# An attention and gated-convolution kernel: one list of operations put in another order from its 149th entry on

## The chip, the cores and the metric

The kernel runs on one core of one Trainium2 chip. The metric is the device time of one execution in microseconds; a kernel's time is the median of its runs. The profiler takes one execution and gives for it a span and, for each instruction, an engine, a start and a duration.

## The reference

Eight batches, eight heads, a sequence of 576 and a head dimension of 64 go through an attention without softmax, a norm over the head dimension, and then a feed-forward block with a depthwise convolution of three taps as its gate. All inputs and the output are float32; the output is 8 x 576 x 512.

```python
kv = np.einsum('bhsd,bhse->bhde', k, v)
out = np.einsum('bhsd,bhde->bhse', q, kv)
rms = np.sqrt(np.mean(out * out, axis=-1, keepdims=True) + 1e-06)
x = out / rms * g_norm                  # then (B, S, H * D) = (8, 576, 512)
...
h = np.maximum(x @ w_in, 0.0)           # 512 -> 1024
for k in range(3):                      # hp: h with a zero row at each end
    conv_out += conv_w[k][None, None, :] * hp[:, k:k + S, :]
gate = 1.0 / (1.0 + np.exp(-conv_out))
y = h * gate @ w_out                    # 1024 -> 512
```

## The kernel before

The kernel has no loop over batches. Some sixty small functions (lines 246 to 777) each issue one step of the work for one batch, half or tile, and a string `ORDER` (lines 59 to 134, 852 tokens) lists the steps. The end of the kernel walks through the list and then ties the instructions of each engine to that order, so that no scheduler moves them:

```python
    for token in ORDER.split():
        what, _, at = token.partition("@")
        slots[:] = [int(s) for s in at.split(",")] if at else []
        name, *args = what.split(".")
        ops[name](*(int(a) if a.isdigit() else a for a in args))
```

A token is a step's name, its arguments, and behind an `@` the places it takes: the PSUM bank (of eight, each 128 x 512 float32; attention steps take two neighbours) or the buffer of a ring. `on.2.1.0@0` is the norm sum of batch 2, head group 1, half 0 of the sequence, in banks 0 and 1. Each engine works through its own instructions in the order of the list; an instruction waits until its inputs are there and until the last reader of its place is done. So the list sets the order of each engine, and the numbers behind `@` set which earlier work a step has to wait for.

The steps of one batch, with the lines under which the profile shows them:

- Loads of q, k and v on GpSimd's queue (`Lq`, `Lk`, `Lv`, L347), each 576 KB and some in two parts.
- On TensorE with quarter arrays (64 x 64): the product of k and v (`kv` L402, 72 matmuls; `kz` L479 for batches 6 and 7), the transposes of q (`qt` L433, 36 matmuls) and the output product (`ot` L460, 4 matmuls; `ox` L500). For batches 6 and 7 q is transposed by a transfer on SyncE's queue instead (`tq` L467), and two transfers swap the halves of the k-v product (`kx` L489). A transfer of this kind stands in SyncE's queue with the stores.
- The copies out of PSUM: `kvd`, `qd` on VectorE (L414, L443), `kva`, `qa` on ScalarE (L416).
- The norm: squares on ScalarE (`sq` L509), the sum over the head dimension as a product with ones on TensorE, either on the whole array (`on` L528, 2 matmuls) or on quarter arrays (`oq` L537, 4 matmuls), the reciprocal root on ScalarE (`nl` L545), and the scaling into x on VectorE (`mo` L556). Batches 4 to 7 take a grouped form (`ss` L566, `ln` L574, `sl` L581 to L584, `sp` L593, `mu` L599) with a copy of the output (`oc` L521).
- The first product of the feed-forward block on TensorE (`hm` L613, `hs` L628, `hk` L658) and its relu on ScalarE (`re` L619, `rh` L640, `rp` L665).
- The gate: two scaled copies and two sums on VectorE (`ta` L681 and L682, `aa` L687, `ab` L692), the sigmoid on ScalarE (`sg` L698), the product with h on VectorE (`mg` L722). Batch 0 takes part of it on TensorE (`cv` L708).
- The second product, two batches at a time in nine tiles of 128 rows (`om` L732; the last tile `oh` L757), the copy of a tile's row out of its bank on ScalarE (`ea` L738, `eh` L767) or VectorE (`ed` L743), and its store on SyncE's queue (`st` L748, `sh` L777).

ScalarE needs one table for the reciprocal root and another for the sigmoid; where the list goes from one to the other, a table load stands in ScalarE's order (L227, ten in all).

In the code the two forms of the norm sum differ in this:

```python
    def on(b, u, s):                                        # L523
        ...
            nc.tensor.matmul(ps[:, tt, :], ones, T["sq", b, u, s][:, tt, :], start=True, stop=True)
    def oq(b, u, s):                                        # L531
        ...
                c = half(i)
                nc.tensor.matmul(
                    ps[c, tt, :], ones[c, c], T["sq", b, u, s][c, tt, :], start=True, stop=True)
```

Of the kernel before, what the change touches and what calls it, by code (L numbers as in the profile page):

```python
# [71 lines left out]
sq.1.0.0@5 hk.0.7.1.0@6 hk.0.7.1.1 rp.7.1 ta.0.1.7@1 ot.1.1.1@0 sq.1.1.1@6 oq.1.0.0@4 nl.1.0.0@5 mo.1.0.0 hk.0.4.0.0@6
hk.0.4.0.1 rp.4.0 hk.0.6.1.0@7 hk.0.6.1.1 rp.6.1 oq.1.1.1@4 nl.1.1.1@6 mo.1.1.1 hk.0.6.0.0@6 Lq.2.0.4@2 hk.0.6.0.1
rp.6.0 ta.0.1.4 hk.1.6.1.0@7 ta.0.1.6 hk.1.0.1.0@2 ot.1.1.0@4 sq.1.1.0@7 aa.0.1.2 hk.1.1.1.0@3 hk.1.2.1.0@6 hk.1.6.1.1
rh.1.6.1 hk.1.1.1.1 rh.1.1.1 on.1.1.0@0 nl.1.1.0@7 mo.1.1.0 hk.1.2.1.1 hk.1.5.1.0@7 hk.1.5.1.1 rh.1.5.1 rh.1.2.1
hk.1.3.1.0@3 hk.1.3.1.1 rh.1.3.1 hk.1.0.1.1 rh.1.0.1 ab.0.1.2 sg.0.1.5 sg.0.1.4 qt.2.1.0@0 qt.2.0.0@6 hk.1.5.0.0@3
hk.1.5.0.1 rh.1.5.0 qd.2.0.0@4 hk.1.0.0.0@2 hk.1.4.1.0@4 hk.1.4.1.1 hk.1.0.0.1 hk.1.1.0.0@5 hk.1.6.0.0@6 hk.1.1.0.1
hk.1.2.0.0@7 hk.1.2.0.1 rh.1.2.0 rh.1.1.0 rh.1.0.0 hk.1.6.0.1 rh.1.6.0 aa.0.1.3 qd.2.1.0@0 ab.0.1.3 sg.0.1.7 sg.0.1.6
hk.1.7.0.0@0 mg.0.1.2 hk.1.7.1.0@1 hk.1.7.1.1 rh.1.7.1 hk.1.7.0.1 rh.1.7.0 ta.1.1.1@0 ta.1.1.0 Lk.2.0.4@1 Lv.2.0.4@0
Lq.3.0.4@0 Lk.3.0.4@0 Lv.3.0.4@1 Lq.4.0.4@1 aa.1.1.0 hk.1.4.0.0@3 om.0.1.0.4@2 rh.1.4.1 hk.1.4.0.1 rh.1.4.0  # L80
om.0.2.0.4@5 kv.2.0.2@6 mg.0.1.3 om.0.1.4.4 ab.1.1.0 sg.1.1.0 sg.1.1.1 kvd.2.0.2@2 ot.2.0.1@0 sq.2.0.1@0 ed.0.1@0
st.0.1 qt.3.1.0@6 qd.3.1.0@1 Lk.4.0.4@1 Lv.4.0.4@0 Lq.5.0.4@2 om.0.2.4.4 on.2.0.1@2 qt.3.0.0@6 qd.3.0.0@2 nl.2.0.1@8
mo.2.0.1@2 om.0.3.0.4@4 ea.0.2@1 ot.2.1.1@6 ot.2.1.0@2 mg.1.1.0 om.0.3.4.4 ed.0.3@2 sq.2.1.0@1 sq.2.1.1@2 on.2.1.0@0
nl.2.1.0@9 mo.2.1.0 om.0.0.0.4@5 hk.1.3.0.0@4 on.2.1.1@0 st.0.2 nl.2.1.1@0 mo.2.1.1 om.0.0.4.4 ed.0.0@3 ot.2.0.0@2
sq.2.0.0@3 hk.1.3.0.1 rh.1.3.0 st.0.0 kv.3.0.2@0 kvd.3.0.2@0 on.2.0.0@6 nl.2.0.0@1 mo.2.0.0 hs.2.0.1@4 rh.2.0.1@1
hs.2.5.1@5 rh.2.5.1 ot.3.1.1@0 sq.3.1.1@4 ta.1.1.5@1 ot.3.0.1@6 sq.3.0.1@5 hs.2.1.1@4 rh.2.1.1 hs.2.4.0@5 rh.2.4.0
ta.1.1.4 ta.1.1.2@0 pn hs.2.4.1@2 rh.2.4.1 hs.2.1.0@3 rh.2.1.0 on.3.1.1@4 nl.3.1.1@2 hs.2.2.0@2 rh.2.2.0 hs.2.5.0@3
rh.2.5.0 on.3.0.1@4 nl.3.0.1@3 aa.1.1.2 mo.3.1.1@0 hs.2.2.1@2 rh.2.2.1 hs.2.0.0@3 rh.2.0.0 ot.3.0.0@0 sq.3.0.0@6
mo.3.0.1 qt.4.0.0@4 qd.4.0.0@3 ta.1.1.3 ab.1.1.2 aa.1.1.1 ot.3.1.0@2 sq.3.1.0@7 hs.2.3.1@6 rh.2.3.1 on.3.0.0@4
nl.3.0.0@4 hs.3.4.1@7 rh.3.4.1 hs.3.1.1@6 rh.3.1.1 on.3.1.0@4 nl.3.1.0@5 mo.3.0.0 hs.3.6.1@7 rh.3.6.1 hs.2.6.0@6  # L90
mo.3.1.0 qt.5.0.0@4 qd.5.0.0@0 ab.1.1.1 qt.4.1.0@0 qd.4.1.0@4 sg.1.1.5 sg.1.1.4 Lq.6.0.4@0 mg.1.1.2 ta.1.1.6@1
ta.1.1.7 aa.1.1.3 hs.2.3.0@7 rh.2.3.0 hs.3.0.1@2 rh.3.0.1 rh.2.6.0 sg.1.1.3 sg.1.1.2 hs.3.7.0@3 hs.3.2.0@4 rh.3.2.0
hs.3.3.0@5 rh.3.3.0 rh.3.7.0 kv.4.0.2@0 kvd.4.0.2@1 hs.3.0.0@2 hs.3.3.1@6 mg.1.1.1 Lk.5.0.4@0 rh.3.3.1 hs.3.2.1@7
rh.3.2.1 hs.3.7.1@4 rh.3.7.1 hs.3.6.0@5 rh.3.6.0 rh.3.0.0 ab.1.1.3 ta.2.2.2@0 ta.2.2.3 hs.3.4.0@3 rh.3.4.0 sg.1.1.7
hs.3.1.0@4 hs.3.5.0@5 sg.1.1.6 rh.3.1.0 qt.5.1.0@0 qd.5.1.0@2 ot.4.0.0@6 sq.4.0.0@0 mg.1.1.3 rh.3.5.0 om.0.7.0.4@2
# [729 lines left out]
```

## Time and profile before

| | |
|---|---|
| timed runs | 177.69, 177.48, 177.60 us; median 177.6 |
| profiled execution, span | 175.6 us (no time of its own is given beside the span) |
| instructions | 5070 |
| TensorE, matmul | 167.9 us busy, 96% |
| TensorE, weight load | 100.0 us, 57% |
| VectorE | 149.5 us, 85% |
| ScalarE | 148.9 us, 85% |
| GpSimd | 22.2 us, 13% |
| DMA | 29.11 MB, mean 166 GB/s |

The shares are means over stages that differ. Up to about 120 us attention and feed-forward work are mixed, with loads up to about 93 us; behind that there is feed-forward work alone, and stores. In the profile's tables a row names the line, the engine, the operation and the tile, then the number of instructions, their busy time, the mean of one in ns, and the idle time ahead of them with what ended it ("issue" is time in which the engine waited for nothing that the profile shows). In a timeline a row gives start, duration, engine, line, and how many instructions are drawn together.

### The profile page before, as it was taken

The page shows a single profiled execution, that of the slowest core. Times are in us where ns is not written, and L with a number is a line of the kernel's source. Part 1 is how long each engine was busy: PE and PEld are TensorE (multiplying, and loading weights), DVE is VectorE, ACT ScalarE, POOL GpSimd, SP SyncE. Part 2 cuts the span into 40 slices and gives each one's busy share as a digit, 9 for nine tenths or more (in the row PEclk, how much of TensorE's full clock was granted, in tenths as well). Part 3 has the DMA queues.
Part 4 walks back from the last instruction along what each step waited for, and adds up shares of the span by engine and source line. Part 5 has one row for each costly group of instructions (what it writes and reads, how often), then busy time and mean ns, then how long its engine had stood idle before and what let it go on. Part 6 is the DMA issues. An engine that isn't in the chain of part 4 may idle for free.

```text
span 175.6 us, 5070 instructions
## 1 busy us (share of the span) xinstructions
PE 167.9 (96%) x2097; PEld 100.0 (57%) x2114; DVE 149.5 (85%) x290; ACT 148.9 (85%) x268; POOL 22.2 (13%) x35
## 2 busy tenths in 40 slices
PE   7979999999999999999999999999999999999992
PEld 2334766676447677644467764444877744444451
DVE  2796638899688899999999998989999999999950
ACT  2368899999978999999999998999999967676721
POOL 3094512200603013030000000000000000000000
PEclk9999999999999999999999999999999999999999
DMA  5999999999999999999999050330310003064486
GB/s 159 392 323 207 207 207 207 208 208 209 207 241 230 227 207 207 170 182 197 258 181 161 14 134 0 119 123 0 119 63 0 0 0 116 13 239 175 179 304 237
DMA packets 25911, 29.11 MB, mean 166 GB/s; under 512 B 6036, under 2 KB 20384, under 8 KB 25888
## 3 DMA queue, kind: packets, MB, share of 16 engines
q0 software_dynamic: 13296, 14.50, 49.2%
q1 hardware_dynamic: 12048, 13.11, 26.2%
q10 hardware_dynamic: 544, 1.18, 1.7%
q8 instruction: 16, 0.26, 0.6%
q14 instruction: 7, 0.06, 0.1%
HBM read 32.52 MB, written 9.44 MB: 239 GB/s over the span
## 4 chain that ended last, share of the span: by engine, by line
PE 76%; DVE 12%; ACT 5%; DMA 3%; issue 3%; ACTq 0%; DVEq 0%
PE banks L732 32%; PE banks L628 14%; PE banks L613 9%; PE banks L658 4%; DMA stg<-in_v_dram 3%; PE banks L460 3%; DVE h L722 2%; PE banks L708 2%; ACT taps L698 2%; PE banks L402 2%; PE banks L593 2%; PE banks L433 1%; PE banks L528 1%; DVE taps L681 1%; PE banks L286 1%
## 5 line engine op out<-in xcount | busy, mean ns | idle before, releaser
L732 PE MATMUL banks<-w_out_sb,h 128*128 128x512 bf16 x267 | 62.8, 379 | 1.2 <-issue 0.6
L698 ACT ACTIVATE taps<-taps,cw 128x576 bf16<-128x576 bf16 (+1 forms) x44 | 40.6, 958 | 5.7 <-DVE taps L692 5.5
L732 PEld LDWEIGHTS <-h 128*128 128x128 bf16 x280 | 26.2, 98 | 30.0 <-issue 1.1
L628 PE MATMUL banks<-x,w_in_sb 128*128 128x288 bf16 (+2 forms) x256 | 34.2, 286 | 0.0
L640 ACT ACTIVATE h<-banks 128x288 bf16<-128x288 f32 (+2 forms) x80 | 29.5, 460 | 0.3 <-PE banks L658 0.2
L628 PEld LDWEIGHTS <-w_in_sb 128*128 128x128 bf16 x256 | 24.4, 98 | 7.8 <-issue 0.8
L722 DVE TENSOR_TENSOR h<-h,taps 128x1152 bf16<-128x1152 bf16 (+1 forms) x24 | 22.8, 952 | 1.2 <-ACT taps L698 1.2
L687 DVE TENSOR_TENSOR taps<-taps 128x1152 bf16<-128x1152 bf16 (+1 forms) x22 | 21.5, 978 | 0.5
L509 ACT ACTIVATE sq<-banks 128x576 bf16<-128x576 f32 (+2 forms) x32 | 20.8, 691 | 1.1 <-PE banks L460 1.1
L692 DVE TENSOR_TENSOR taps<-taps,h 128x1152 bf16<-128x1152 bf16 (+1 forms) x22 | 21.4, 972 | 0.3
L681 DVE TENSOR_SCALAR taps<-h,cw 128x576 bf16<-128x576 bf16 (+1 forms) x44 | 18.7, 424 | 0.6 <-ACT h L665 0.5
L682 DVE TENSOR_SCALAR taps<-h,cw 128x576 bf16<-128x576 bf16 (+1 forms) x44 | 18.4, 418 | 0.0
L738 ACT ACTIVATE row<-banks 128x512 f32<-128x512 f32 x23 | 13.5, 597 | 5.7 <-PE banks L732 4.2
L658 PE MATMUL banks<-x,w_in_sb 128*128 128x288 bf16 (+2 forms) x128 | 17.7, 286 | 0.1
L613 PE MATMUL banks<-x,w_in_sb 128*128 128x288 bf16 x128 | 16.9, 286 | 0.0
L556 DVE SCALAR_TENSOR_TENSOR x<-banks,cw,rs 128x576 bf16<-128x576 f32 (+2 forms) x16 | 13.0, 816 | 3.9 <-ACT rs L545 3.6
L658 PEld LDWEIGHTS <-w_in_sb 128*128 128x128 bf16 x128 | 12.0, 98 | 4.4 <-issue 0.5
L227 ACT ACT_TABLE_LOAD x10 | 12.8, 1283 | 2.0 <-issue 1.8
L613 PEld LDWEIGHTS <-w_in_sb 128*128 128x128 bf16 x128 | 12.3, 98 | 3.7 <-issue 0.2
L443 DVE COPY qT<-banks 128x1152 bf16<-128x1152 bf16 (+2 forms) x13 | 8.8, 681 | 5.7 <-PE banks L433 5.7
L545 ACT ACTIVATE rs<-banks,eps_sb 128x576 f32<-128x576 f32 (+2 forms) x16 | 11.8, 740 | 1.1 <-PE banks L528 1.1
L599 DVE SCALAR_TENSOR_TENSOR x<-o,cw,banks 128x576 bf16<-128x576 f32 (+2 forms) x16 | 12.1, 810 | 0.7 <-PE banks L593 0.5
(89 smaller groups left out, 162.9 us busy)
## 6 DMA issues: line engine op xcount, KB each, us to landing
out_dram<-row SPq DMA_DIRECT2D x35, 256.0 KB, 2.3
q_sb<-in_q_dram POOLq DMA_DIRECT2D x6, 576.0 KB, 17.9
k_sb<-in_k_dram POOLq DMA_DIRECT2D x6, 576.0 KB, 14.5
v_sb<-in_v_dram POOLq DMA_DIRECT2D x6, 576.0 KB, 17.9
stg<-in_v_dram ACTq DMA_DIRECT2D x2, 576.0 KB, 6.2
stg<-in_k_dram SPq DMA_DIRECT2D x4, 288.0 KB, 6.9
w_in_sb<-in_moe_w_in_dram POOLq DMA_DIRECT2D x2, 512.0 KB, 9.9
w_out_sb<-in_moe_w_out_dram POOLq DMA_DIRECT2D x1, 1024.0 KB, 15.5
```

Source lines behind the costliest of these rows:

```text
L509: nc.scalar.activation(T["sq", b, u, s], T["o", b, u, s], AX.Square)
L613: nc.tensor.matmul(ps[:, s, :HS], w_in_sb[:, t, f * P:(f + 1) * P], T["x", b][:, t, c0:c1], start=(t == 0), stop=(t == NT - 1))
L628: nc.tensor.matmul(ps, w_in_sb[:, t, f * P:(f + 1) * P], T["x", b][:, t, c0:c1], start=(t == 0), stop=(t == NT - 1))
L640: nc.scalar.activation(h, fr, AX.Relu)
L658: nc.tensor.matmul(T[at], w_in_sb[:, t, f * P:(f + 1) * P], T["x", b][:, t, c0:c1], start=(t == 0), stop=(t == NT - 1))
L681: nc.vector.tensor_scalar_mul(tap[:, 0, f % 2, :n, 8:8 + S], h[:, f], cw[:, f:f + 1])
L682: nc.vector.tensor_scalar_mul(tap[:, 1, f % 2, :n, :S], h[:, f], cw[:, 2 * NF + f:2 * NF + f + 1])
L687: nc.vector.tensor_add(tap[:, 1, :, :n, :S], tap[:, 0, :, :n, 7:7 + S], tap[:, 1, :, :n, 1:1 + S])
L692: nc.vector.tensor_add(y, y, span(b, n)[:, 2 * j:2 * j + 2])
L698: nc.scalar.activation(y, y, AX.Sigmoid, scale=cw[:, NF + f:NF + f + 1])
L722: nc.vector.tensor_mul(h, h, tap_of(b, j)[:, 1, :, :n, :S])
L732: nc.tensor.matmul(T["om", p, m], h[:, f, m * P:(m + 1) * P], w_out_sb[:, f, :], start=(f == 0), stop=(f == NF - 1))
```

## The change

The first 148 entries of the list are written in another order too, but give each engine the same row of steps, up to about 30 us. The entries behind them are put in another order that moves steps on every engine, and the numbers of banks and buffers are assigned anew. The functions and all line numbers stay. The steps themselves differ in a few places only: three norm sums change their form (`oq.1.0.0` and `oq.1.1.1` become `on`, `on.2.1.0` becomes `oq`), and eight tiles change the engine that copies them (`ea.0.2`, `ea.3.1` to VectorE's `ed` and, the other way, `ed.0.0`, `ed.1.8` and others; VectorE has 12 copies before and 10 after, ScalarE 23 and 25). One line of the list, of before and of after, from the end:

```diff
-mg.7.1.3 om.3.3.0.4@2 om.3.3.4.4 ed.3.3@5 st.3.3 mg.7.1.2 om.3.1.0.4@1 om.3.2.0.4@7 om.3.0.4.4 om.3.2.4.4 ed.3.2@0
+ea.3.0@4 st.3.0 st.3.1 st.3.2 sg.7.1.5 mg.7.1.2 om.3.7.4.4 ed.3.7@0 om.3.5.4.4 ea.3.5@1 om.3.4.4.4 ea.3.4@2 st.3.5
```

What this does to the engines' orders is shown at three places. The first is VectorE in batch 3's norm, from the first sum of one pair of gate taps of batch 1 (L687) to the gate product of that pair (L722, taps_73), before:

```order
L687 TENSOR_TENSOR taps_73<-taps_73 128x2x576
L556 SCALAR_TENSOR_TENSOR x<-banks,cw,rs 128x2x288 x2
L443 COPY qT<-banks 128x1152
L681 TENSOR_SCALAR taps_72<-h,cw 128x576
L682 TENSOR_SCALAR taps_72<-h,cw 128x576
L692 TENSOR_TENSOR taps_73<-taps_73,h 128x2x576
L687 TENSOR_TENSOR taps_72<-taps_72 128x2x576
L556 SCALAR_TENSOR_TENSOR x<-banks,cw,rs 128x2x288 x2
L443 COPY qT<-banks 128x1152
L692 TENSOR_TENSOR taps_72<-taps_72,h 128x2x576
L443 COPY qT<-banks 128x1152
L722 TENSOR_TENSOR h<-h,taps_73 128x2x576
```

and after:

```order
L687 TENSOR_TENSOR taps_73<-taps_73 128x2x576
L681 TENSOR_SCALAR taps_72<-h,cw 128x576
L682 TENSOR_SCALAR taps_72<-h,cw 128x576
L556 SCALAR_TENSOR_TENSOR x<-banks,cw,rs 128x2x288 x2
L692 TENSOR_TENSOR taps_73<-taps_73,h 128x2x576
L687 TENSOR_TENSOR taps_72<-taps_72 128x2x576
L556 SCALAR_TENSOR_TENSOR x<-banks,cw,rs 128x2x288
L692 TENSOR_TENSOR taps_72<-taps_72,h 128x2x576
L556 SCALAR_TENSOR_TENSOR x<-banks,cw,rs 128x2x288
L443 COPY qT<-banks 128x1152 x2
L722 TENSOR_TENSOR h<-h,taps_73 128x2x576
```

L556 is the scaling of a norm half into x, L443 the copy of transposed q, L681 and L682 the scaled copies of the gate, L692 its second sum. Before, the first two halves were scaled directly behind the first L687, and the copies of q stood between the pairs; now two gate copies stand ahead of them, the last two halves are scaled one by one with L692 between them, and two copies of q stand together ahead of the product.

The second place is TensorE in batch 2's norm: the norm sum L528 of one half, ahead of it the second product of the feed-forward block (L732). Before, from the last product on:

```order
L732 LDWEIGHTS h
L732 MATMUL banks<-w_out_sb,h 128x512
L658 LDWEIGHTS w_in_sb
L658 MATMUL banks<-x,w_in_sb 128x288
L658 LDWEIGHTS w_in_sb
L658 MATMUL banks<-x,w_in_sb 128x288
L528 LDWEIGHTS ones
L528 MATMUL banks<-sq,ones 128x288
L528 LDWEIGHTS ones
L528 MATMUL banks<-sq,ones 128x288
```

and after, from the sum of the half ahead on:

```order
L537 LDWEIGHTS ones
L537 MATMUL banks<-sq,ones 64x288
L732 LDWEIGHTS h
L732 MATMUL banks<-w_out_sb,h 128x512
L732 LDWEIGHTS h
L732 MATMUL banks<-w_out_sb,h 128x512
L732 LDWEIGHTS h
L732 MATMUL banks<-w_out_sb,h 128x512
L732 LDWEIGHTS h
L732 MATMUL banks<-w_out_sb,h 128x512
L528 LDWEIGHTS ones
L528 MATMUL banks<-sq,ones 128x288
```

The sum of the half ahead is now in the quarter-array form (L537), and the two products of L658 that stood between are elsewhere.

The third place is SyncE's queue, behind the first loads: the stores (L748), the transposing transfers of q of batches 6 and 7 (L467) and the swaps of their k-v product (L489). Before:

```order
L748 DMA out_dram<-row 128x512 x3
L467 DMA_TRANSPOSE qT<-q_sb 128x9x128
L748 DMA out_dram<-row 128x512 x3
L489 DMA kvx<-kvb 64x256 x2
L467 DMA_TRANSPOSE qT<-q_sb 128x9x128 x2
L748 DMA out_dram<-row 128x512
L489 DMA kvx<-kvb 64x256 x2
L748 DMA out_dram<-row 128x512
L467 DMA_TRANSPOSE qT<-q_sb 128x9x128
L748 DMA out_dram<-row 128x512 x27
```

and after:

```order
L748 DMA out_dram<-row 128x512 x4
L467 DMA_TRANSPOSE qT<-q_sb 128x9x128
L748 DMA out_dram<-row 128x512
L489 DMA kvx<-kvb 64x256 x2
L748 DMA out_dram<-row 128x512 x2
L467 DMA_TRANSPOSE qT<-q_sb 128x9x128 x3
L489 DMA kvx<-kvb 64x256 x2
L748 DMA out_dram<-row 128x512 x28
```

Behind the first transposing transfer there were three stores, a swap and then two more such transfers; now there are one store, a swap, two stores and three transposing transfers in a row.

148 lines of the change are left out of this document (74 added, 74 removed).

## The prediction

> **What bounds the kernel now.** I read the page's busy shares first, then the windows view over eight stretches, then the chain of waits, the waits by engine, and the timelines of VectorE, ScalarE and SyncE.
>
> ```profile
> PE 167.9 (96%) x2097; PEld 100.0 (57%) x2114; DVE 149.5 (85%) x290; ACT 148.9 (85%) x268; POOL 22.2 (13%) x35
> 30.00:53.00 23.00, 22.54 (x434) 14.34 (x436) 19.09 (x34) 21.27 (x42) 4.76 (x7) 1.00 1.20 215
> 53.00:67.00 14.00, 13.96 (x251) 10.06 (x241) 12.57 (x28) 13.46 (x30) 2.22 (x3) 1.00 1.20 219
> 67.00:87.00 20.00, 19.58 (x387) 11.00 (x384) 19.46 (x35) 19.94 (x40) 2.96 (x4) 1.00 1.24 202
> 87.00:120.00 33.00, 32.67 (x313) 19.55 (x315) 30.98 (x43) 32.46 (x51) 0.00 (x0) 1.00 0.54 103
> 120.00:167.00 47.00, 46.70 (x283) 26.96 (x284) 46.16 (x82) 38.77 (x70) 0.00 (x0) 1.00 0.23 86
> ```
>
> In a window the columns are its length, then the busy time of PE, weight load, DVE, ACT and POOL, the granted clock, the DMA share and GB/s. TensorE is busy nearly all the time at full clock: from 30 to 167 us it is idle for 0.46 + 0.04 + 0.42 + 0.33 + 0.30 = 1.55 us. But VectorE is hardly freer. From 67 us on it idles for 0.54 + 2.02 + 0.84 = 3.40 us in 100, and before that 1.43 us (53 to 67) and 3.91 us (30 to 53). Both engines therefore set the time, which the end of the timeline shows:
>
> ```profile
> 165.31 0.69 DVE L743 COPY row<-banks 128x512 f32<-128x512 f32 x1
> 165.91 0.75 DVE L722 TENSOR_TENSOR h<-h,taps 128x1152 bf16<-128x1152 bf16 x1
> 166.71 3.23 PEld L732 LDWEIGHTS <-h 128*128 128x128 bf16 x16 [0.22 <-DVE h L722]
> ```
>
> VectorE's last gate product (L722, 165.91 to 166.66) releases the last piece of the output product on TensorE (L732 at 166.71). Whatever makes VectorE's queue later up to that product, and isn't won back in a gap, makes the end later; so does whatever makes TensorE's queue longer. The larger of the two delays counts, not their sum.
>
> The profiled execution has a span of 175.6 us, and the median of the three timed runs is 177.6: some 2.0 us lie around the span. I work in differences and add them to 177.6.
>
> **The change part by part.** It is one list of tokens in another order with other bank and buffer numbers; three norm sums change their form and eight evictions their engine, and nothing else is added or removed. The engines' orders agree up to some 30 us. So the costs are changes of tile shape on TensorE, new waits for banks, work shifted between VectorE and ScalarE, and queue order on SyncE and GpSimd.
>
> *TensorE, shape changes.* The short products of the attention (L402, L433, L460, L537) use quarter arrays; the rest uses whole ones. Each change into quarter arrays stands in the waits as time without a releaser:
>
> ```profile
> PEld L460 <- issue: 3.4, 10, 0.5
> PEld L402 <- issue: 1.7, 6, 0.4
> PEld L433 <- issue: 1.6, 6, 0.4
> 31.78 0.43 PE banks L537 x4
> 49.40 0.24 PE banks L528 x2
> ```
>
> That is 3.4 / 10 = 0.34 us for each at L460, 0.28 at L402 and 0.27 at L433. Counted in the two orders, behind 30 us there are 31 stretches of quarter-array products before and 34 after. The three come at the output products of batch 4, the k-v product of batch 6 and the grouped norm of batch 7, all behind 67 us. They cost 3 x 0.34 = 1.02 us; the bounds are 0 (if the gap is filled by matmuls still streaming) and 3 x 0.5 = 1.5. I take 0.34 because the stretches that are split begin with L460, whose mean is the nearest row. Two norm sums change from the four-matmul form (L537) to the two-matmul form (L528) and one changes back, so one fewer: 0.24 - 0.43 = -0.19.
>
> The Trainium skill, "TensorEngine Tiling (Array Packing)", Key Properties, says that changing the tiling mode drains the array, which the rows above bear out; "TensorE: Matmul & The Clock Gate", Single matmul latency, puts a drain near 175 ns. By that figure, an estimate, the three would cost 0.53 instead of 1.02; the trace's 0.34 decides here.
>
> *TensorE, bank waits around batch 2 (43 to 53 us).* The new list takes the lowest free bank again and again. The sum for the half 2.1.0 (now L537) and that for 2.1.1 (L528) stand in bank 6 with only four output products between them, where before there were also two L658 products.
>
> ```profile
> 49.65 0.86 PE banks L732 x4
> 48.48 1.19 ACT L509 ACTIVATE sq<-banks 128x576 bf16<-128x576 f32 x2
> 49.69 0.74 ACT L545 ACTIVATE rs<-banks,eps_sb 128x576 f32<-128x576 f32 x1
> ```
>
> The second sum has to wait until ScalarE has read the first (L545, 0.74 us). That read stands behind the second square, half of 1.19, of which the sum of 0.43 covers most. From the first square's end the read ends at 0.60 + 0.74 = 1.34, plus some 0.2 for two hand-overs; the four products cover up to 0.10 + 0.43 + 0.86 = 1.39. The wait is some 0.15 to 0.35; bounds 0 and 0.74. The sum for 2.0.1 stands directly behind its square with less between (some 0.2), and the output product for 2.1.0 waits in bank 2 for an eviction (some 0.2). Together 0.7, bounds 0 and 2 x 0.74. The TensorE sum is 1.02 - 0.19 + 0.7 = +1.5 us.
>
> *VectorE, batch 3 (54 to 67 us).* Before, the chain of waits ran from here into VectorE's full stretch; the first row is ScalarE's timeline, the next two are the chain, then VectorE's timeline and the weight load's:
>
> ```profile
> 57.28 0.73 ACT L545 ACTIVATE rs<-banks,eps_sb 128x576 f32<-128x576 f32 x1
> 65.04 1.45 ACT taps L698 x2
> 66.51 0.76 DVE h L722
> 56.74 0.27 DVE L336 TENSOR_REDUCE ng<-ident 128x1 f32<-128x32 bf16 x2
> 44.87 0.49 PEld L433 LDWEIGHTS <-q_sb 64*64 64x64 bf16 x36
> ```
>
> ScalarE's read of the first norm sum of batch 3 (L545 at 57.28) opens a row of work that has no room: in the window from 53 to 67 us ScalarE is busy for 13.46 of 14.00 us. It ends in the two sigmoids (L698), which release VectorE's gate product at 66.51, behind which VectorE's queue is nearly full. The new order sets a group of 36 transposes of q, those of batch 4, ahead of that first sum (they stood behind two of the sums); such a group took 0.49 us. With what TensorE lost up to there, 0.7 - 0.19 = 0.5 (the additional shape changes all come later), the first sum is 1.0 late, and so is everything behind it on ScalarE up to the sigmoids. The bounds are 0.3, if the bank waits are nothing and ScalarE finds relu work to bring forward, and 0.49 + 1.48 - 0.19 = 1.8 with the waits at their upper end. VectorE has no cover: the taps of this gate are done by then. The five small operations of L336 to L339, which began at 56.74 and filled a wait there, now stand right behind the place where the orders part.
>
> *Evictions.* Of the output rows VectorE now copies nine ahead of its last gate product, where it copied eight; one more is 0.69 us by the row of L743 above, in a queue without room. In all it copies two fewer, but those go from behind the product, where it has time. Bounds 0 and 0.69 x 2; I take 0.69.
>
> *What is won back.* Waits of VectorE behind 66.51 can absorb lateness:
>
> ```profile
> DVE h L722 <- ACT taps L698: 1.2, 3, 0.7
> DVE x L599 <- PE banks L593: 0.5, 1, 0.5
> DVE hi L581 <- ACT rs L574: 0.3, 1, 0.3
> ```
>
> That is 2.0, less 0.24 at 66.51 itself, so 1.8 at most. But what VectorE waits for there comes from TensorE and ScalarE, late by 1.5 as well; I take 0.1. VectorE's sum is 1.0 + 0.69 - 0.1 = +1.6 us, a little more than TensorE's +1.5. The larger gives **177.6 + 1.6 = 179.2 us**.
>
> *Queues.* SyncE now issues two stores ahead of the second transposing transfer of batch 6 (L467):
>
> ```profile
> 86.91 5.98 SPq L467 DMA_TRANSPOSE qT<-q_sb  x2
> qT<-q_sb SPq DMA_TRANSPOSE x4, 8.2
> 87.40 0.58 ACT L738 ACTIVATE row<-banks 128x512 f32<-128x512 f32 x1
> 100.38 0.58 SPq L748 DMA_DIRECT2D out_dram<-row  x1
> 96.28 0.30 PE L500 MATMUL banks<-qT,kvx 64*64 64x256 bf16 x4
> ```
>
> The second of those stores waits for the copy that ended at 87.40 + 0.58 = 87.98; its issue takes 0.58, so the transfer starts at 88.6 instead of 86.91 and lands 8.2 later, at 96.8. Its reader ran at 96.28: 0.5 late against the old times, and hidden if TensorE is 1.5 late by then. I put it at nothing, and at 0.5 if TensorE is on time. The loads on GpSimd's queue change places (k of batches 5 and 6 ahead of q of the next); the last load is the same, and I put it at nothing, bounds -0.3 and +0.3.
>
> By the Trainium skill, "DMA: Bandwidth & Descriptors", Latency and other measured facts, a transposing transfer reaches 261 GB/s; 128 x 9 x 128 bf16 is 295 KB, so an estimate of 1.1 us would leave no wait here at all. The 8.2 of the trace speaks against it.
>
> **The rivals.** A difference of 0.2% (0.36 us) is about what a measurement of this kernel can tell from none.
>
> *Faster.* The new list may do better where VectorE idles: 1.43 + 3.40 = 4.83 us behind 53 us. If evictions and norm steps come where they are due and a third of that goes, with the shape changes hidden, the time is 177.6 - 1.6 = 176.0; a small success lies at 177.0. For it: waits for ScalarE (L722 1.2, L556 before that) depend on order alone. Against it: TensorE has only 1.55 us of gaps and gets three more stretches.
>
> *No change.* The 1.8 us of waits absorb the 1.7 that VectorE loses: 177.5. It needs TensorE's loss below 0.4.
>
> *Transfer late.* If TensorE is not late at 96 us by itself, or the transfer takes longer because three now stand in a row, its reader adds 0.5 to 0.8 to VectorE's loss: 180.0.
>
> *Tight banks everywhere.* If the turn of the banks stalls at each norm of batches 2 and 3 (eight halves, 0.3 us each, 2.4 us) on top of the 1.6, then 181.6. It decides if waits for L545 and L509 at L528 and L460 pass 2 us. Against it: only two such turns are visible without slack.
>
> **How the numbers follow.** Chances: forecast 0.47 (its own range 178.0 to 180.0), transfer late 0.10, tight banks 0.16, no change 0.07, faster 0.20. The low end 176.9 leaves out about half of the faster case (0.1), and the high end 181.6 about half of the tight banks (0.08). Faster 0.20, same 0.07, slower 0.73.
>
> **What would show it.** Right: L722's product that stood at 66.51 starts 0.8 to 1.3 later than before; VectorE's last L722 ends at about 168.3 and TensorE waits for it; the idle time of L460, L433 and L402 in the weight load grows by about a us. Wrong: TensorE level with before at 66 us; or the product at 66.51 on time and VectorE idling less than 3.4 us behind it; or an idle stretch at 96 us put down to the transposing transfer.

## The result and the profile after

The time went from 177.64 us (4 runs) to 178.32 us (4 runs): a ratio of 1.0042 [1.0028, 1.0056], or +0.68 us. The profiled execution of the new kernel took 178.32 us with a span of 176.5, where the span before was 175.6. The direction is the one forecast. The size is less than half of the +1.6 forecast.

The busy shares hardly moved (TensorE 95%, VectorE 84%, ScalarE 85%). The windows view, with the same stretches as in the prediction:

```profile
30.00:53.00 23.00, 22.49 (x396) 14.31 (x400) 19.72 (x39) 20.86 (x42) 3.96 (x6) 1.00 1.21 208
53.00:67.00 14.00, 13.91 (x248) 9.97 (x249) 11.63 (x20) 13.20 (x28) 2.23 (x3) 1.00 1.18 239
67.00:87.00 20.00, 19.41 (x385) 10.81 (x388) 19.23 (x33) 19.94 (x42) 3.71 (x5) 1.00 1.21 190
87.00:120.00 33.00, 32.77 (x314) 19.19 (x315) 31.47 (x43) 31.93 (x50) 0.00 (x0) 1.00 0.47 117
120.00:167.00 47.00, 46.84 (x285) 27.03 (x288) 46.30 (x82) 40.55 (x72) 0.00 (x0) 1.00 0.23 87
```

VectorE idles more than before between 53 and 87 us (2.37 + 0.77 against 1.43 + 0.54) and yet the end is later: it is not VectorE that sets it there. TensorE idles for 0.51 + 0.09 + 0.59 + 0.23 + 0.16 = 1.58 us from 30 to 167, as against 1.55 before. The column that stands out is ScalarE's from 67 to 87: 19.94 of 20.00 us busy, in both kernels. An engine without a gap can hand lateness on but not win it back. That holds of ScalarE up to 87 us only: behind it ScalarE idles for 1.07 us of 33 and for 6.45 of 47, TensorE for 0.23 and 0.16.

ScalarE's timeline of the new kernel shows the lateness at three points; the rows of before stood at 57.28, 65.04 and 87.40:

```profile
56.60 0.65 ACT L509 ACTIVATE sq<-banks 128x576 bf16<-128x576 f32 x1 [0.20 <-PE banks L460]
57.99 0.73 ACT L545 ACTIVATE rs<-banks,eps_sb 128x576 f32<-128x576 f32 x1
65.61 1.44 ACT L698 ACTIVATE taps<-taps,cw 128x576 bf16<-128x576 bf16 x2
87.96 0.58 ACT L738 ACTIVATE row<-banks 128x512 f32<-128x512 f32 x1
```

That is +0.71 at the first norm sum of batch 3, +0.57 at the sigmoids and +0.56 at the eviction of tile 0.6. The new kernel's timeline at its end (weight load, VectorE, TensorE; rows that overlap are of different engines) goes on from there:

```profile
163.97 6.57 PEld L732 LDWEIGHTS <-h 128*128 128x128 bf16 x31
166.23 0.76 DVE L722 TENSOR_TENSOR h<-h,taps 128x1152 bf16<-128x1152 bf16 x1
170.87 1.91 PE L757 MATMUL banks<-w_out_sb,h 128*128 128x256 bf16 x16
```

and before, TensorE's last products stood here:

```profile
170.28 1.91 PE L757 MATMUL banks<-w_out_sb,h 128*128 128x256 bf16 x16
```

TensorE's last products are 0.59 later. The last gate product ends at 166.23 + 0.76 = 166.99, and the weight load runs on without a wait in front of it, where before it waited 0.22 for that product. How TensorE came to be late shows in its weight load, at places where both lists have done the same products; first before, then the new kernel:

```profile
74.74 0.55 PEld L732 LDWEIGHTS <-h 128*128 128x128 bf16 x4
114.56 3.13 PEld L732 LDWEIGHTS <-h 128*128 128x128 bf16 x16 [0.24 <-issue]
121.08 1.41 PEld L732 LDWEIGHTS <-h 128*128 128x128 bf16 x8
```

```profile
75.35 0.55 PEld L732 LDWEIGHTS <-h 128*128 128x128 bf16 x4
115.38 3.14 PEld L732 LDWEIGHTS <-h 128*128 128x128 bf16 x16 [0.24 <-issue]
121.68 1.41 PEld L732 LDWEIGHTS <-h 128*128 128x128 bf16 x8
```

That is +0.61, +0.82 and +0.60. Between these places it is +0.55 from 62 to 70 us, +0.69 at 77 and +0.84 from 90 to 112. So the 0.59 at the end is not ScalarE's 0.57 handed on unchanged, near as the two numbers are. TensorE loses another 0.2 between 75 and 90 us, which no run isolates, and wins 0.2 back between 118 and 121 us. Two runs below, in which the new list from 104 us on follows the old front, show that gain by itself (0.25 and 0.23).

**Where the 0.71 comes from.** TensorE was about 0.25 late at 52 us, with batch 3's second group of transposes of q still to come, which before was done by then. The chain of waits of the new kernel between 52 and 60 us shows what else stands ahead of that first sum:

```profile
55.05 0.31 PE banks L433 x36
55.96 0.41 PE banks L433 x36
56.37 0.19 PE banks L460 x4
57.99 0.73 ACT rs L545
```

These are two groups of transposes (L433). The first is that of batch 3, which stood at 44.87 us before; the second is batch 4's, which stood at 59.46, behind the first sums. Both are now ahead of the output product (L460) that the sum needs. The weight loads of batch 3's group and of that product, then VectorE's copy of the group, without which the product can't run:

```profile
54.76 0.49 PEld L433 LDWEIGHTS <-q_sb 64*64 64x64 bf16 x36
56.16 0.19 PEld L460 LDWEIGHTS <-kvb 64*64 64x64 bf16 x4
```

```profile
55.43 0.76 DVE L443 COPY qT<-banks 128x1152 bf16<-128x1152 bf16 x1
```

The weight load of that output product stood at 54.43 before, so it came 1.73 later, and the square behind it (L509 at 56.60, with 0.20 of waiting for L460) followed. The copy ended at 55.43 + 0.76 = 56.19, just ahead of the product, so either group holds the product by itself: batch 4's on TensorE, batch 3's through the copy. That is read from the trace. Two runs below take away one group each; one wins nothing at the sum, the other 0.26 of the 0.71. None takes away both.

### The profile page after: what moved, and what is told of

The parts are those of the page before. It is cut to its first block, busy times and chain, and to the rows that moved or that the text cites. A ratio compares the mean times of both kernels' runs of the same rounds, so it can differ in the third digit from the quotient of the medians.

```text
span 176.5 us, 5052 instructions
## 1 busy us (share of the span) xinstructions
PE 168.2 (95%) x2095; PEld 99.7 (56%) x2112; DVE 147.8 (84%) x288; ACT 150.1 (85%) x270; POOL 22.2 (13%) x35
## 4 chain that ended last, share of the span: by engine, by line
PE 73%; DVE 12%; ACT 6%; issue 3%; DMA 3%; ACTq 0%
PE banks L732 30%; PE banks L628 11%; PE banks L613 9%; PE banks L658 8%; DMA stg<-in_v_dram 3%; ACT rs L545 2%; PE banks L433 2%; PE banks L708 2%; PE banks L460 2%; DVE qT L443 2%; DVE taps L687 2%; DVE taps L682 2%; PE banks L286 1%; PE banks L402 1%; PE banks L593 1%
## 5 line engine op out<-in xcount | busy, mean ns | idle before, releaser
L732 PE MATMUL banks<-w_out_sb,h 128*128 128x512 bf16 x267 | 63.1, 380 | 1.0 <-issue 0.5
L732 PEld LDWEIGHTS <-h 128*128 128x128 bf16 x280 | 26.1, 98 | 30.2 <-issue 1.6
L640 ACT ACTIVATE h<-banks 128x288 bf16<-128x288 f32 (+2 forms) x80 | 30.2, 472 | 1.4 <-PE banks L628 0.8
L722 DVE TENSOR_TENSOR h<-h,taps 128x1152 bf16<-128x1152 bf16 (+1 forms) x24 | 22.8, 952 | 2.0 <-ACT taps L698 1.9
L509 ACT ACTIVATE sq<-banks 128x576 bf16<-128x576 f32 (+2 forms) x32 | 20.9, 700 | 1.8 <-PE banks L460 1.7
L687 DVE TENSOR_TENSOR taps<-taps 128x1152 bf16<-128x1152 bf16 (+1 forms) x22 | 21.5, 976 | 0.5
L692 DVE TENSOR_TENSOR taps<-taps,h 128x1152 bf16<-128x1152 bf16 (+1 forms) x22 | 21.3, 970 | 0.2
L681 DVE TENSOR_SCALAR taps<-h,cw 128x576 bf16<-128x576 bf16 (+1 forms) x44 | 18.6, 422 | 0.6 <-ACT h L665 0.6
L682 DVE TENSOR_SCALAR taps<-h,cw 128x576 bf16<-128x576 bf16 (+1 forms) x44 | 18.9, 430 | 0.0
L738 ACT ACTIVATE row<-banks 128x512 f32<-128x512 f32 x25 | 14.5, 599 | 5.0 <-PE banks L732 4.9
L658 PE MATMUL banks<-x,w_in_sb 128*128 128x288 bf16 (+2 forms) x128 | 17.5, 286 | 0.1
L556 DVE SCALAR_TENSOR_TENSOR x<-banks,cw,rs 128x576 bf16<-128x576 f32 (+2 forms) x16 | 13.0, 815 | 3.6 <-ACT rs L545 3.5
L658 PEld LDWEIGHTS <-w_in_sb 128*128 128x128 bf16 x128 | 12.2, 98 | 4.0
L599 DVE SCALAR_TENSOR_TENSOR x<-o,cw,banks 128x576 bf16<-128x576 f32 (+2 forms) x16 | 12.2, 810 | 1.4 <-PE banks L593 1.1
L443 DVE COPY qT<-banks 128x1152 bf16<-128x1152 bf16 (+2 forms) x13 | 8.8, 681 | 5.3 <-PE banks L433 5.3
```

Source lines behind the costliest of these rows:

```text
L509: nc.scalar.activation(T["sq", b, u, s], T["o", b, u, s], AX.Square)
L640: nc.scalar.activation(h, fr, AX.Relu)
L658: nc.tensor.matmul(T[at], w_in_sb[:, t, f * P:(f + 1) * P], T["x", b][:, t, c0:c1], start=(t == 0), stop=(t == NT - 1))
L681: nc.vector.tensor_scalar_mul(tap[:, 0, f % 2, :n, 8:8 + S], h[:, f], cw[:, f:f + 1])
L682: nc.vector.tensor_scalar_mul(tap[:, 1, f % 2, :n, :S], h[:, f], cw[:, 2 * NF + f:2 * NF + f + 1])
L687: nc.vector.tensor_add(tap[:, 1, :, :n, :S], tap[:, 0, :, :n, 7:7 + S], tap[:, 1, :, :n, 1:1 + S])
```

## The experiments

The working theory after the result: the late start of batch 3 is handed on by ScalarE to the end. Its rivals were VectorE's sum with its evictions (the forecast's own step), the stretches of quarter arrays, and the bank waits of batch 2. All times stand beside runs of the kernel before that were taken with them (177.55 to 177.64 us); differences to the new kernel are against 178.32. "New" and "old" are the lists after and before.

### Undoing parts of the new list

**Two evictions back on ScalarE.**

```diff
-ed.1.8@4
+ea.1.8@4
...
-ed.3.1@1
+ea.3.1@1
```

> The new order with two evictions given back from VectorE to ScalarE (tiles 1.8 and 3.1; slots and places in the list unchanged). Theory A, TensorE's queue sets the end and VectorE's extra evictions are hidden in its waits: 178.3, within 0.2. Theory B, VectorE sets the end and each eviction ahead of its last gate product counts: 0.69 to 1.38 less, 177.0 to 177.6.

Measured 180.59 us, 1.0172 [1.0158, 1.0186]: 2.27 slower than the new kernel, where one theory expected no change and the other, VectorE's load, a gain. ScalarE's timeline and the weight load's show it:

```profile
120.13 1.08 ACT L738 ACTIVATE row<-banks 128x512 f32<-128x512 f32 x2 [1.24 <-DMA out_dram<-row]
169.52 0.55 PEld L732 LDWEIGHTS <-h 128*128 128x128 bf16 x4 [1.17 <-DVE h L722]
```

ScalarE waits for the store of an earlier row to free a row buffer, by 1.24 here and by 1.00 once more at 166.27, and TensorE ends up waiting 1.17 for the last gate product. The buffers have the same numbers as in the new kernel. But ScalarE copies tile 1.8 at 116.73, where VectorE did at 112.56, and in the list its store stands ahead of the store that frees the buffer of the first wait. That, not the 0.6 us of the copy, set the price. What VectorE's additional copies cost the new kernel this run can't say.

**Stretches joined.** Four steps moved so that four stretches of small products (quarter arrays, and L593, which takes 32 rows of the array) join a neighbour; two of them:

```diff
-ot.4.0.0@2 hs.3.5.0@4
+hs.3.5.0@4 ot.4.0.0@2
...
-sp.7.1.1.6@6 mu.6.0.1@0 mu.6.1.1 sp.7.0.0.6@4 om.1.5.4.4
+om.1.5.4.4 sp.7.1.1.6@6 mu.6.0.1@0 mu.6.1.1 sp.7.0.0.6@4
```

> The new order with four stretches of quarter-array products joined to a neighbour by moving one TensorE step each (35 stretches become 31; VectorE's and ScalarE's orders unchanged). Theory A, TensorE sets the end and a stretch costs some 0.25: 4 x 0.25 less, 177.3 to 177.6. Theory B, VectorE sets the end: 178.3, within 0.2.

Measured 179.18 us, 1.0094 [1.0078, 1.0109], 0.86 slower than the new kernel and outside both expectations. The waits from 118 to 124 us:

```profile
PEld L593 <- issue: 1.5, 2, 1.1
PE banks L593 <- DVE x L599: 0.8, 1, 0.8
```

In the new kernel the first row reads 0.8 and the second is not there. The whole-array products that split the stretch had filled a wait for VectorE's read of the bank; without them TensorE stands for 0.78 us and goes, against the new kernel, from 0.12 to 0.84 late. Here the change of tile shape that the join saves cost nothing, and the other three joins up to 118 us had won nothing either.

**Halves of the lists.** New up to 104 us and old behind it, and the reverse.

> The new order up to the 557th entry (about 104 us, where both lists have done the same steps), then the old one. In the trace of the new order TensorE is 0.84 late there. Theory A: that stays, 178.2 to 178.6. Theory B: VectorE, 0.9 late there, has no extra evictions behind it and wins back 0.5 to 0.8: 177.7 to 178.0.

> The old order up to the 557th entry (about 104 us), then the new one. Theory A: in the new order's tail TensorE's lateness shrank from 0.84 to 0.59, so 0.25 less than before, 177.3 to 177.6. Theory B: the tail has one eviction more on VectorE, 0.69 more than before: 178.2 to 178.4.

New front, old tail: 179.41 us, 1.0105 [1.0090, 1.0121], more than either list alone and than both theories expected. Its waits from 104 to 118 us show the seam, behind which nine steps had to be given other banks or buffers (ten in the reverse run):

```profile
PE banks L500 <- ACT row L738: 0.5, 1, 0.5
```

ScalarE's copy of an output row (L738) frees the bank late, and TensorE goes, against before, from 0.91 to 1.60 late at 109 to 113 us. Old front, new tail: 178.14 us, 1.0033 [1.0020, 1.0046], but a span of 175.7 and TensorE's last products at 170.03, 0.25 earlier than before. Inside the span the new tail costs next to nothing here. The time is +0.59 all the same, close to what the theory of VectorE's copies expected, but not by VectorE: its last gate product ends at 166.17, 0.49 earlier than before. The loss lies around the span (178.00 - 175.7 = 2.3 us, 2.0 before and 1.8 in the new kernel). Why, stays open.

**Middle and end.** The old list with the new entries 557 to 833; and the new list with the last 18 entries of the old.

> The old order, but from the 557th to the 833rd entry (104 to 166 us) the new one; the last stores and copies are the old order's. Theory: the new middle brings TensorE 0.24 forward, and the time over that of the old order in the run with the new tail came from the new order's end alone (its last store came 0.33 later behind the last product): 177.2 to 177.4. Rival, the middle itself costs time that the span doesn't show: 177.9 to 178.2.

> The new order with the old order's last 18 entries (behind 166 us: one copy on VectorE instead of ScalarE, the order of the last stores and of the two half tiles). Theory: 0.2 to 0.4 less, 177.9 to 178.1. Rival, the end doesn't matter: 178.3.

The first: 177.72 us, 1.0004 [0.9996, 1.0013], with TensorE's last products at 170.05, again 0.23 earlier without a gain in time; 177.2 to 177.4 was expected, or 177.9 to 178.2 by the rival. So the new order from 104 us to shortly before the end costs nothing by itself. The second: 178.76 us, 1.0063 [1.0051, 1.0075], 0.44 slower than the new kernel: the end of the new list suits it better than the old end would, and the expectation was missed.

**New up to 69 us, then old.**

> The new order up to the 387th entry (69 us), then the old one. The new order is 0.57 late there on ScalarE and VectorE. If lateness at 69 us is handed on in full, 178.1 to 178.2; if the old order's waits behind it (1.8 us in all on VectorE) win it back, 177.6 to 177.8.

Measured 184.39 us, 1.0368 [1.0336, 1.0399]. Its waits show that the run is spoiled for this question, by the mixed order of the loads: TensorE stands still once for 4.3 us, at L479, for a load of v.

**Bank wait of batch 2 filled.** A product is moved ahead of the norm sum that had only four products in front of it:

```diff
-on.2.1.1@6 nl.2.1.1@1 mo.2.1.0 om.0.0.4.4
+om.0.0.4.4 on.2.1.1@6 nl.2.1.1@1 mo.2.1.0
```

> The new order with four output products of tile 0.0 moved ahead of batch 2's norm sum 2.1.1, so that they fill its bank wait (some 0.35). If bank waits of TensorE cost what the prediction says (theory A): 178.0. Theory C: the sum and ScalarE's read of it come some 0.5 later, so no gain: 178.3 to 178.8.

Measured 178.78 us, 1.0066 [1.0053, 1.0079], 0.46 slower than the new kernel. The waits from 46 to 54 us:

```profile
ACT rs L545 <- PE banks L528: 1.0, 1, 1.0
```

The sum comes later and ScalarE waits 1.0 us for it, 0.5 in the new kernel; the first sum of batch 3 comes 0.41 later. Filling TensorE's wait cost time there instead of saving it.

**Transposes moved.** Those of batch 4 put back behind the first sums (the step that the forecast had priced at 0.49), and those of batch 3 put early again (the second cut shows where they are put in):

```diff
-qt.4.0.0@2 qd.3.1.0@0 ot.3.1.1@6
+qd.3.1.0@0 ot.3.1.1@6
...
-hs.3.6.1@0 rh.2.3.0
+hs.3.6.1@0 qt.4.0.0@6 rh.2.3.0
```

> The new order with the transposes of batch 4 (36, and VectorE's copy of them, 0.67) moved back behind batch 3's norm sums. The prediction's step: the first sum comes 0.4 to 0.5 earlier and with it the gate product, 177.8 to 177.9. Theory C': the copy had stood in an idle time of VectorE and now stands ahead of the gate product, where VectorE is on the chain, so nothing is won: 178.3 to 178.6.

```diff
-om.0.3.0.4@1 ed.0.2@1 mo.2.0.1@0
+om.0.3.0.4@1 qt.3.1.0@6 ed.0.2@1 mo.2.0.1@0 qd.3.1.0@4
```

> The new order with batch 3's own second group of transposes (36, and VectorE's copy of them) moved back from 55 us to 46 us, as in the old order. Theory D: batch 3's first output product waits for just this copy, and the first norm sum, ScalarE's row behind it and the gate product follow; so 0.3 to 0.5 less, 177.8 to 178.0. The prediction's step (batch 4's group is what delays the sum): no change, 178.3.

Batch 4's: 179.70 us, 1.0118 [1.0103, 1.0132], slower than both expectations, and the first sum of batch 3 was not earlier. Its output product waits for VectorE's copy of batch 3's group instead, by TensorE's timeline; and batch 4's group, at its late place, makes the next group wait in the same bank, by the waits from 60 to 69 us:

```profile
56.38 0.32 PE L460 MATMUL banks<-qT,kvb 64*64 64x288 bf16 x4 [0.28 <-DVE qT L443]
PE banks L433 <- DVE qT L443: 0.6, 1, 0.6
```

So batch 4's group costs that sum nothing as long as batch 3's stands in front of it too.

Batch 3's: 179.89 us, 1.0128 [1.0113, 1.0142], slower than both expectations. TensorE's timeline shows that the group behind it had to wait for the copy in the one bank that was to be had, before the place in question is reached:

```profile
49.13 0.48 PE L433 MATMUL banks<-ident,q_sb 64*64 64x64 bf16 x36 [0.89 <-DVE qT L443]
```

Against the new kernel TensorE was 1.36 late there and the first sum 1.10 late; 0.26 was won back on the way, less than the 0.71 asked for. The copy of batch 3's group was long done by then (49.08), but in the chain of waits batch 4's group (57.06 to 57.54) stands right ahead of the output product. So batch 3's group alone does not explain the late sum either. The run set two groups one behind the other into the same banks; others were not tried.

### One eviction to VectorE, in either list

```diff
-ea.0.6@4
+ed.0.6@4
```

> The new order with the eviction of tile 0.6 (ScalarE, at 88 us) given to VectorE, nothing else. Theory C, ScalarE is the queue without room from 61 to 110 us and hands its lateness on: 0.3 to 0.6 less, 177.7 to 178.0. Theory B, VectorE sets the end: 0.69 more, 178.9 to 179.0. Theory A, TensorE's own queue: 178.3.

> The old order with the same single eviction (tile 0.6, ScalarE, at 87 us) given to VectorE. Theory C: 0.3 to 0.6 less, 177.0 to 177.3. Theory B: 178.2. Theory A: 177.6.

(In the old list the buffer is 3.) In the new list 179.21 us, 1.0089 [1.0074, 1.0103], +0.89 on the new kernel; in the old one 177.95 us, 1.0020 [1.0011, 1.0029], +0.35. So the working theory failed its own test, in both lists: 0.6 us less on ScalarE at 88 us won nothing. VectorE copies the row at 88.68 in the new list's version. The last scaling into x of this norm in its timeline, then the same one in the new kernel:

```profile
93.87 0.81 DVE L599 SCALAR_TENSOR_TENSOR x<-o,cw,banks 128x576 bf16<-128x576 f32 x1
```

```profile
93.19 0.81 DVE L599 SCALAR_TENSOR_TENSOR x<-o,cw,banks 128x576 bf16<-128x576 f32 x1
```

The scaling into x (L599) comes 0.68 later, the length of one copy, and TensorE's last products are 0.67 later. The forecast's price of an eviction is right at this place, where the copy stands right ahead of work that TensorE needs next; in the old list it stands among the same scalings and costs half of that.

### Prices by place, each put into the old list

**VectorE, 0.6 us of work** (the five small operations L336 to L339, done a second time) ahead of the gate product at 66.51, ahead of `sl.6` at 116 us, and ahead of the last gate product but one at 164 us:

```diff
-mg.1.1.2
+pn mg.1.1.2
```

> The old order with the five small VectorE operations of L336 to L339 (0.6 to 0.7 us) run a second time right ahead of the gate product at 66.5 us, nothing else: a late start of VectorE's full stretch by itself. The prediction's step (0.1 won back behind it): 0.5 to 0.6 more than before, 178.1 to 178.2. Theory E (lateness is won back between 104 and 160 us where VectorE waits for others, unless TensorE took it over): 0.1 to 0.4 more, 177.7 to 178.0.

> The same five operations a second time at 116 us, ahead of L581, where VectorE waits 0.39 for ScalarE and 0.45 for TensorE in the trace. The prediction's price, work on VectorE ahead of its last gate product counts in full wherever it stands: 0.6 to 0.7 more, 178.2 to 178.3. Theory E (place decides): 0 to 0.3 more, 177.6 to 177.9.

> The same five operations a second time at 164.6 us, ahead of VectorE's last gate product but one, for whose successor TensorE waits. Both theories: 0.5 to 0.7 more, 178.1 to 178.3. If TensorE's 0.22 of waiting there isn't VectorE's: 177.6.

At 66 us: 177.69 us, 1.0002 [0.9994, 1.0011]. VectorE's timeline shows the lateness put on and gone:

```profile
66.93 0.75 DVE L722 TENSOR_TENSOR h<-h,taps 128x1152 bf16<-128x1152 bf16 x1
85.38 0.42 DVE L414 CAST kvb<-banks 128x256 bf16<-128x256 f32 x1 [0.24 <-PE banks L479]
```

Before, these rows stood at 66.51 and 85.19. The operations take 0.62 us, of which a part fills a wait. From 69 us on VectorE is 0.54 late, 0.12 of which is an offset that the whole profile has: 0.42 was put on. At 85 us 0.19 is left, and from 92 us on the offset alone. TensorE was never more than 0.1 late beyond the offset. The time is +0.08, and its interval includes no change. At 116 us it is +0.22, 177.83 us, 1.0012 [1.0003, 1.0021]; at 164 us +0.53, 178.14 us, 1.0029 [1.0018, 1.0040], where TensorE waits for the product by the timeline:

```profile
167.22 0.76 PEld L732 LDWEIGHTS <-h 128*128 128x128 bf16 x5 [0.85 <-DVE h L722]
```

The same 0.62 us cost next to nothing, a third or most of their length, by what stands behind them.

**TensorE, one change of tile shape** in the late stretch where TensorE is full:

```diff
-sp.6.1.0.6@4 mu.6.1.0 hs.7.2.0@6
+hs.7.2.0@6 sp.6.1.0.6@4 mu.6.1.0
```

> The old order with one L628 step set between the two grouped norm steps (L593) at 129.7 us, where TensorE has no gap: one stretch of other tile shapes more, nothing else. The prediction's price of a stretch: 0.34 more, 177.9 to 178.0. Rival, a stretch costs nothing even here: 177.6.

Measured 177.82 us, 1.0011 [1.0002, 1.0019], +0.21 us. The weight load's timeline, and then that of before:

```profile
129.68 0.10 PEld L593 LDWEIGHTS <-spread 32*128 32x128 bf16 x2 [0.21 <-issue]
130.57 0.09 PEld L593 LDWEIGHTS <-spread 32*128 32x128 bf16 x2 [0.26 <-issue]
```

```profile
129.66 0.10 PEld L593 LDWEIGHTS <-spread 32*128 32x128 bf16 x4 [0.21 <-issue]
```

The second stretch adds a gap of 0.26. TensorE is 0.35 late directly behind it, and 0.24 from 134 us to the end.

**ScalarE, some 0.6 us of work** (two relus done a second time, same input and output) ahead of its full stretch at 60 us, and at 131 us:

```diff
-rh.2.2.1 hs.2.0.0@3 rh.2.0.0
+rh.2.2.1 hs.2.0.0@3 rh.2.0.0 rh.2.2.1 rh.2.0.0
```

> The old order with two relu steps of ScalarE (L640, some 0.6 us in all) run a second time at 60 us, ahead of batch 3's third square: lateness of ScalarE by itself in the stretch where it has no gap (19.94 of 20.00 us busy from 67 to 87). Theory F, this is how the new order's 0.57 at 67 us was handed on: 0.4 to 0.6 more than before, 178.0 to 178.2. Rival, it is won back as VectorE's is: 177.6 to 177.8.

> The same kind of extra work (two relu steps of L640 a second time, some 0.6 us) on ScalarE at 133 us, where it has gaps (38.77 of 47 us busy from 120 to 167). Theory F: 0 to 0.1 more, 177.6 to 177.7. Rival, work on ScalarE counts wherever it stands: 0.4 to 0.6 more.

At 60 us: 177.99 us, 1.0019 [1.0010, 1.0028], +0.35, a little under what was expected. ScalarE's timeline:

```profile
65.38 0.78 ACT L698 ACTIVATE taps<-taps,cw 128x576 bf16<-128x576 bf16 x1
```

Against before that is +0.34 at the sigmoid (65.04), +0.32 at the eviction of tile 0.6, +0.32 at TensorE's last products and +0.35 in the time. By these points the lateness of ScalarE at 65 us arrives whole at the end, while that of VectorE at 66.5 was won back. But the run makes TensorE late at the same place: the repeated relus read banks that an output product behind them needs. The waits from 57 to 68 us, then TensorE's weight load far behind:

```profile
PE banks L460 <- ACT h L640: 0.2, 1, 0.2
114.88 3.13 PEld L732 LDWEIGHTS <-h 128*128 128x128 bf16 x16 [0.24 <-issue]
```

The last row stood at 114.56 before, +0.32; from 62 us on TensorE is 0.32 to 0.39 late throughout. Whether ScalarE or TensorE carries the delay up to 87 us this run doesn't show. From 120 us on it can't be ScalarE, which idles for 7.91 of 47 us there.

At 131 us: 178.94 us, 1.0075 [1.0062, 1.0087], where nothing to 0.1 was expected. The waits say why:

```profile
PE banks L628 <- ACT h L640: 1.4, 1, 1.4
```

The second read holds a bank 1.9 us longer, and TensorE waits 1.4 for it. This is the price of a bank held, not of ScalarE's work, and says nothing about ScalarE at that place.

In the seven runs on the old list that leave its last stretch as it is, the time follows TensorE's last products (L757, 170.28 before):

| added to the old list | last products | time |
|---|---|---|
| VectorE's work at 66 us | +0.11 | +0.08 |
| VectorE's work at 116 us | +0.22 | +0.22 |
| VectorE's work at 164 us | +0.41 | +0.53 |
| one more stretch of L593 at 130 us | +0.24 | +0.21 |
| eviction to VectorE at 87 us | +0.27 | +0.35 |
| ScalarE's work at 60 us | +0.32 | +0.35 |
| ScalarE's work at 131 us | +1.46 | +1.30 |

No kernel that was run is faster than the one before.

## Why the prediction was right or wrong

**The direction** was right, and so was the place where the delay begins, the first sum of batch 3. The rest of the sum failed in five steps. That the time lies between 178.0 and 180.0 is owed to the width of that range: its middle, 179.2, is 0.9 too high.

1. *VectorE's sum as the one that sets the end* (late start 1.0, evictions 0.69, won back 0.1; +1.6). This is the step that failed. The run with 0.42 put on VectorE at 66.5 us in the old list ended with +0.08, so VectorE does win back what it loses there; and in the new kernel TensorE no longer waits for VectorE's last gate product. In its place TensorE sets the end: 0.61 late at 75 us, 0.84 from 90 to 112 and 0.59 at its last products, for 0.68 in the time. To leave VectorE out would not have saved the forecast, though, since TensorE's own sum was +1.5; that one was too large by the steps 4 and 5. The gate product stood at 67.08 instead of 66.51, +0.57, where I said 0.8 to 1.3; the late start was 0.71 at the sum and 0.57 at the sigmoids that release the product.
2. *The source of the late start.* I charged 0.5 for what TensorE had lost and 0.49 for batch 4's transposes. TensorE was about 0.25 late at 52 us, and the other 0.46 came behind it, so the second size was near. But I had overlooked batch 3's own second group, moved from 44.87 to 54.76. Each of the two groups holds the output product by itself: taking batch 4's away won nothing, taking batch 3's away 0.26. Which share each has stays open.
3. *One eviction more, 0.69.* Tile 1.8 goes from ScalarE to VectorE (the section on the change lists it among those that go the other way). In the new kernel its copy stands at 112.56, for 0.69. TensorE's lateness doesn't grow behind it (0.84 at 112 us, 0.82 at 115), so no cost is to be seen; no run measures it alone. Work of 0.6 us on VectorE cost 0.08, 0.22 and 0.53 by its place, an eviction to VectorE 0.89 in the new list at 88.7 us and 0.35 in the old.
4. *Shape changes, 3 x 0.34.* One stretch more of the 32-row form, where TensorE is full, measured 0.35 directly behind it, 0.24 farther on and 0.21 in the time. The three of the sum no run isolates. Over the stretches in which they stand, with other moved steps, TensorE went from 0.55 to 0.61 (70 to 75 us), from 0.69 to 0.84 (77 to 90) and from 0.82 to 0.60 (115 to 121); to join the last one again cost 0.72. The lower bound, 0, was the nearer one. The Trainium skill's figure for a drain ("TensorE: Matmul & The Clock Gate", Single matmul latency), near 175 ns, is closer to the 0.24 that stayed than the 0.34 that I took from the rows; directly behind the stretch the rows were right.
5. *Bank waits of batch 2, 0.7.* In the new kernel's timeline only one of the three stands as a wait of TensorE, at the lower end of the 0.15 to 0.35 that I gave it:

```profile
50.86 0.41 PE L528 MATMUL banks<-sq,ones 128*128 128x288 bf16 x2 [0.18 <-ACT rs L545]
```

So the tight banks of the rival, more than 2 us of such waits, didn't come either. The gaps of the quarter arrays and two of VectorE's waits, in the new kernel's waits:

```profile
PEld L460 <- issue: 4.2, 12, 0.5
...
DVE h L722 <- ACT taps L698: 1.9, 3, 0.8
...
PEld L433 <- issue: 1.6, 6, 0.4
...
PEld L402 <- issue: 1.1, 4, 0.4
...
DVE x L599 <- PE banks L593: 1.1, 2, 0.6
```

The three gaps together are 6.9 us, 6.7 before: +0.2, where I expected about a us. VectorE waits more for others (L722 1.9 against 1.2, L599 1.1 against 0.5), which is an engine that is being kept waiting, not one that sets the end.

**The test at the end** that I had named failed as well: VectorE's last product was to end near 168.3 with TensorE waiting for it; it ended at 166.99, and TensorE didn't wait.

**The queues** cost nothing, as said, for a better reason than the one given. The timeline of the new kernel (SyncE's queue and TensorE), then its DMA view, whose last column is the median from issue to landing:

```profile
89.00 5.28 SPq L467 DMA_TRANSPOSE qT<-q_sb  x3
97.87 0.30 PE L500 MATMUL banks<-qT,kvx 64*64 64x256 bf16 x4
```

```profile
qT<-q_sb SPq DMA_TRANSPOSE x4, 4.8
```

The three transposing transfers start at 89.00, later than the 88.6 of the sum, but the median from issue to landing is 4.8 us and not 8.2, and their reader doesn't wait: TensorE is as late behind it as ahead of it, 0.84. The rival of a late transfer fell with that.

**What is shown and what is argued.** Shown: 0.42 us put on VectorE at 66.5 us doesn't reach the end, so the forecast's step is wrong; and where the end of the list is left alone, the time follows TensorE's last products. Shown too: the new list from 104 us on wins TensorE some 0.2 back, by which its 0.84 becomes 0.59. Argued from the trace alone: that the two moved groups of transposes make the first sum late. Open: whether ScalarE or TensorE carries the delay from 57 to 87 us, where TensorE loses the 0.2 behind 75 us, and what happens behind the last products. There the entries 557 to 833 of the new list on the old front lose again the 0.23 that TensorE had won, so the 0.59 of the last products and the 0.68 of the time agree only within that.

## What to carry to other kernels

Follow a delay to the engine that has no gap up to the end, and ask whether it makes that engine late. Here it is TensorE, idle for 1.6 us in 137: what made it late stayed, and 0.42 us on VectorE that didn't make it late cost 0.08. Price a moved step by what it holds (a bank, a row buffer) and by what stands right behind it, not by its length: the same 0.6 us on VectorE cost 0.08, 0.22 or 0.53, a 0.7 us eviction 0.35 or 0.89, and two evictions whose stores came late 2.27. And a list that has been fitted as a whole resists single edits: a run that takes one part back measures the new collision as much as the part, and where two parts hold the same step, taking back either shows little.

## What the runs showed of the hardware that was not expected

- The time around the span is not constant: 2.0 us before, 1.8 in the new kernel, 2.3 with the old front and the new tail. From the end of the last store's issue to the end of the timed run it was 4.6 to 5.2 us. A gain of 0.23 in TensorE's end can vanish there.
- The four transposing transfers landed in a median of 4.8 us where three were issued in a row, as against 8.2 where stores and swaps stood between.
- One more change from whole-array products to the 32-row form of L593 cost TensorE 0.24 us in a full stretch (0.35 directly behind it), and nothing where TensorE would have waited anyway.
